# A transformer block with sliding-window attention: key-major scores, column-tiled PV, DMA layout changes and a list scheduler

## Chip, cores, metric

One core of a Trainium2 chip. The metric is the device time of one execution in microseconds, median of several runs.

## The reference

2048 tokens of 640 channels, all bf16; 32 heads of 20 channels; each query sees itself and the 255 keys before it; a gated MLP of width 1536. Shift, scale and gate vectors come from a vector `c` through `w_mod`.

```python
mod = (_silu(c) @ w_mod).reshape(c.shape[0], 6, 1, -1)      # sa, ca, ga, sb, cb, gb
h = _layernorm(x) * (1 + ca) + sa
q, k, v = h @ wqkv                                          # per head: 2048 x 20
scores = q @ k.T * 20 ** -0.5                               # masked to 0 <= i - j < 256
x = x + ga * ((softmax(scores) @ v) @ wo)
h = _layernorm(x) * (1 + cb) + sb
x = x + gb * ((_sigmoid(h @ w_gate) * (h @ w_up)) @ w_down)
```

## The kernel before

Tokens stand in 16 blocks of 128. A small planner (`Sched`) records each operation in program order on its engine, derives the semaphore waits, and emits five instruction streams; the order within an engine is the order of the Python code.

`ln1_stats` and `ln1_trans` normalise four blocks on VectorE (`xh`, L464), transpose them by TensorE matmuls with an identity into `ps_M`, and scale and shift them on the way out (`hT`, L492). `proj_tasks` computes Q and K transposed, with each head padded from 20 to 32 rows (`wq_pad`, `wk_pad`), so that head 4g + j of group g lies on partitions 32j to 32j + 19 (L590 evicts), and V with tokens on partitions, 22 columns a head, one of them ones (`vaug`, L605).

`attn_block(i)` handles one query block. For each four heads twelve score matmuls (three key blocks by four heads, L299) put keys on partitions: the stationary operand is a K block, 20 rows of one row group, the moving operand the 128 queries. ScalarE exponentiates two heads at a time (L730), GpSimd masks the far key block (L734), VectorE the diagonal one (L738). PV is query-major: the exponentiated block, 128 x 128, is stationary, V's 21 columns move, and three matmuls a head accumulate in `ps_O`. At the end of a block VectorE divides by the sums (L757, L758), TensorE transposes the result (L766), ScalarE evicts it (`oT`, L769), two groups of five matmuls apply `wo`, and VectorE adds the residual (L778).

The MLP of a chunk of four blocks (two for the last two chunks) starts after its attention: gate and up in 24 groups of five matmuls (L633 evicts gate by tanh, L640 multiplies), then down in two groups of twelve matmuls a block, a residual addition (L656) and the store (L660).

Attention and the rest are interleaved by hand: after each pair of heads `run_fill` takes one task from `fillq` (a projection group, a transpose, an MLP group) if it is due (`not_before` counts pairs). Nothing is left to take when `fillq` is empty or its tasks aren't due. All of `ps_M`'s users share two banks; the scores have four banks, PV two. Helper lines are L298 and L299 for all matmuls. All 31 DMAs are issued by SyncE: 15 loads at the start and one store a block.

Of the kernel before, what the change touches and what calls it, by code (L numbers as in the profile page):

```python
# [12 lines left out]

class Res:
    __slots__ = ("name", "w", "r", "psum")

    def __init__(self, name, psum=False):
        self.name = name  # L20
        self.w = None
        self.r = []
        self.psum = psum


class Op:
    __slots__ = ("fn", "waits", "skey", "inc", "tag")

    def __init__(self, fn, waits, skey, inc, tag=""):
        self.fn = fn  # L30
        self.waits = waits
        self.skey = skey
        self.inc = inc
        self.tag = tag


class Sched:
    ENG = ("pe", "act", "dve", "pool", "sp")
    ENGATTR = {"pe": "tensor", "act": "scalar", "dve": "vector", "pool": "gpsimd", "sp": "sync"}
    NDMA = 8  # L40

    def __init__(self, nc):
        self.nc = nc
        self.ops = {e: [] for e in self.ENG}
        self.cnt = {e: 0 for e in self.ENG}
        for k in range(self.NDMA):
            self.cnt[f"d{k}"] = 0
        self.cnt["out"] = 0
        self.dma_last = {f"d{k}": None for k in range(self.NDMA)}
        self.dma_rr = 0  # L50
        self.waited = {e: {} for e in self.ENG}
        self.tag = ""

    def add(self, eng, fn, reads=(), writes=(), signal=True, skey=None, inc=1, extra=()):
        key = skey or eng
        deps = {}

        def dep(ev, res=None):
            if ev is None:
                return  # L60
            k, v = ev
            if res is not None and res.psum and k == key:
                return
            if deps.get(k, 0) < v:
                deps[k] = v

        for r in reads:
            if r.w is None:
                raise RuntimeError(f"resource {r.name} read before any write (program order violation)")
            dep(r.w, r)  # L70
        for w in writes:
            dep(w.w, w)
            for ev in w.r:
                dep(ev, w)
        for ev in extra:
            dep(ev)
        waits = []
        wd = self.waited[eng]
        for k, v in deps.items():
            if k == key and v > self.cnt[k]:  # L80
                raise RuntimeError(f"engine {eng} depends on its own unsignaled op ({k},{v})")
            if wd.get(k, 0) < v:
                waits.append((k, v))
                wd[k] = v
        if signal:
            self.cnt[key] += inc
            ev = (key, self.cnt[key])
            op = Op(fn, waits, key, inc, self.tag)
        else:
            ev = (key, self.cnt[key] + inc)  # L90
            op = Op(fn, waits, None, 0, self.tag)
        self.ops[eng].append(op)
        for r in reads:
            r.r.append(ev)
        for w in writes:
            w.w = ev
            w.r = []
        return ev

    def dma(self, fn, reads=(), writes=()):  # L100
        k = f"d{self.dma_rr}"
        self.dma_rr = (self.dma_rr + 1) % self.NDMA
        prev = self.dma_last[k]
        ev = self.add("sp", fn, reads=reads, writes=writes, signal=True, skey=k, inc=16,
                      extra=([prev] if prev is not None else ()))
        self.dma_last[k] = ev
        return ev
# [38 lines left out]
D = 640  # L146
H = 32
# [734 lines left out]
```

## Time and profile before

| | |
|---|---|
| time, median of three runs | 559.47 us (559.28 to 560.45) |
| span of the profiled execution | 557.5 us |
| busy: PE, ACT, DVE, POOL | 423.9, 281.2, 262.8, 133.2 us |
| mean granted TensorE clock | 0.881 of 2.4 GHz |

The span runs from the first to the last instruction of one profiled execution; the time of a run takes in what lies around it. PE is TensorE's matmuls, PEld its weight loads (they overlap matmuls), DVE is VectorE, ACT ScalarE, POOL GpSimd, SP SyncE. The end of a matmul is modelled, so start to start tells more than a duration. A share is an average over stages with different limits.

### The profile page before, as it was taken

The page shows a single profiled execution, that of the slowest core. Times are in us where ns is not written, and L with a number is a line of the kernel's source. Part 1 is how long each engine was busy: PE and PEld are TensorE (multiplying, and loading weights), DVE is VectorE, ACT ScalarE, POOL GpSimd, SP SyncE. Part 2 cuts the span into 40 slices and gives each one's busy share as a digit, 9 for nine tenths or more (in the row PEclk, how much of TensorE's full clock was granted, in tenths as well). Part 3 has the DMA queues.
Part 4 walks back from the last instruction along what each step waited for, and adds up shares of the span by engine and source line. Part 5 has one row for each costly group of instructions (what it writes and reads, how often), then busy time and mean ns, then how long its engine had stood idle before and what let it go on. Part 6 is the DMA issues. An engine that isn't in the chain of part 4 may idle for free.

```text
span 557.5 us, 11493 instructions
## 1 busy us (share of the span) xinstructions
PE 423.9 (76%) x4784; PEld 254.3 (46%) x4828; DVE 262.8 (47%) x701; ACT 281.2 (50%) x441; POOL 133.2 (24%) x249
## 2 busy tenths in 40 slices
PE   0686789846597798985567889898557887984997
PEld 0333355424354454653344445655334445662665
DVE  5685432274473443435674444322844465445232
ACT  5112567755486666537355657267645564470120
POOL 4004800232222222314122313032323222230000
PEclk9987999975599999997558999999756999997899
DMA  8994000000000000010000000000000000100000
GB/s 288 358 393 162 1 2 1 1 1 2 2 1 1 1 1 2 14 36 1 1 1 1 2 1 1 25 25 2 2 1 1 1 2 2 36 13 1 1 25 25
DMA packets 12580, 20.07 MB, mean 36 GB/s; under 512 B 1136, under 2 KB 9968, under 8 KB 12528
## 3 DMA queue, kind: packets, MB, share of 16 engines
q1 hardware_dynamic: 12528, 19.34, 9.8%
q8 instruction: 38, 0.62, 0.4%
q14 instruction: 14, 0.11, 0.1%
HBM read 16.71 MB, written 2.62 MB: 35 GB/s over the span
## 4 chain that ended last, share of the span: by engine, by line
PE 59%; DVE 17%; ACT 13%; issue 7%; DMA 2%; POOL 1%; SPq 0%; ACTq 0%; POOLq 0%; DVEq 0%
PE ps_M L298 50%; ACT arena L730 8%; PE ps_S L299 6%; DVE stats L432 4%; PE ps_O L298 3%; DVE arena L738 2%; DMA arena<-in_w_mod_dram 2%; ACT oT L769 2%; DVE hT L492 2%; ACT arena L590 1%; DVE xh L464 1%; DVE arena L640 1%; PE ps_M L766 1%; DVE mvb L434 1%; POOL arena L734 1%
## 5 line engine op out<-in xcount | busy, mean ns | idle before, releaser
L730 ACT ACTIVATE arena<-ps_S 128x768 bf16<-128x768 f32 (+2 forms) x256 | 189.8, 768 | 100.9 <-PE ps_S L299 99.6
L734 POOL TENSOR_SCALAR_AFFINE_SELECT arena<-arena 128x256 bf16<-128x256 bf16 x224 | 109.7, 490 | 320.7 <-ACT arena L730 320.7
L738 DVE TENSOR_TENSOR arena<-arena,masku 128x256 bf16<-128x256 bf16 x256 | 81.5, 318 | 169.3 <-ACT arena L730 168.9
L298 PEld LDWEIGHTS ps_O<-vaug,arena 128*128 128x128 bf16 x1440 | 68.1, 100 | 56.2 <-DVE arena L738 15.6
L298 PE MATMUL ps_O<-vaug,arena 128*128 128x21 bf16 x1440 | 74.7, 176 | 18.6 <-DVE arena L738 13.4
L299 PE MATMUL ps_S<-arena 20*128 20x128 bf16 x1440 | 47.8, 239 | 36.9 <-ACT arena L730 30.6
L298 PE MATMUL ps_M<-h2T,wu_sb 128*128 128x512 bf16 (+1 forms) x294 | 64.0, 350 | 2.4 <-issue 0.8
L633 ACT ACTIVATE sig<-ps_M 128x512 f32<-128x512 f32 (+1 forms) x60 | 30.7, 512 | 69.7 <-PE ps_M L298 65.1
L298 PE MATMUL ps_M<-h2T,wg_sb 128*128 128x512 bf16 (+1 forms) x287 | 61.9, 347 | 4.8 <-DVE h2T L492 2.9
L590 ACT ACTIVATE arena<-ps_M 128x512 bf16<-128x512 f32 x64 | 38.2, 597 | 44.6 <-PE ps_M L298 43.8
L298 PE MATMUL ps_M<-wd_sb,arena 128*128 128x320 bf16 x384 | 55.6, 299 | 2.7 <-DVE arena L640 2.4
L299 PEld LDWEIGHTS ps_S<-arena 20*128 20x128 bf16 x1440 | 23.4, 99 | 54.6 <-ACT arena L730 38.3
L640 DVE SCALAR_TENSOR_TENSOR arena<-sig,ps_M 128x512 bf16<-128x512 f32 (+1 forms) x60 | 34.6, 577 | 20.0 <-PE ps_M L298 19.9
L298 PE MATMUL ps_M<-hT,wq_pad 128*128 128x512 bf16 x143 | 39.6, 407 | 5.6 <-DVE arena L738 1.7
L298 PEld LDWEIGHTS ps_M<-wd_sb,arena 128*128 128x128 bf16 x384 | 35.9, 98 | 17.6 <-DVE arena L640 3.2
L298 PE MATMUL ps_M<-hT,wk_pad 128*128 128x512 bf16 x152 | 40.8, 400 | 2.1 <-issue 0.8
L298 PE MATMUL ps_M<-wo_sb,oT 128*128 128x320 bf16 x160 | 29.8, 343 | 13.4 <-ACT oT L769 13.4
L298 PEld LDWEIGHTS ps_M<-h2T,wu_sb 128*128 128x128 bf16 x300 | 26.2, 101 | 23.3 <-DVE arena L640 5.0
L298 PEld LDWEIGHTS ps_M<-h2T,wg_sb 128*128 128x128 bf16 x300 | 26.8, 101 | 21.5 <-DVE h2T L492 2.1
L778 DVE TENSOR_TENSOR x_sb<-ps_M,x_sb 128x320 bf16<-128x320 f32 x32 | 15.7, 491 | 43.8 <-PE ps_M L298 43.8
L298 PE MATMUL ps_M<-ident,xh 128*128 128x128 bf16 x160 | 21.4, 267 | 19.4 <-DVE xh L464 5.3
L432 DVE BATCH_NORM_STATS2 stats<-x_sb 128x6 f32<-128x320 bf16 x64 | 31.0, 485 | 2.7 <-DMA x_sb<-in_A_x_dram 1.6
(56 smaller groups left out, 303.5 us busy)
## 6 DMA issues: line engine op xcount, KB each, us to landing
x_sb<-in_A_x_dram SPq DMA_DIRECT2D x4, 640.0 KB, 11.4
out_dram<-x_sb SPq DMA_DIRECT2D x16, 160.0 KB, 1.8
arena<-in_w_mod_dram SPq DMA_DIRECT2D x1, 2400.0 KB, 9.4
wg_sb<-in_B_w_gate_dram SPq DMA_DIRECT2D x1, 1920.0 KB, 16.7
wu_sb<-in_B_w_up_dram SPq DMA_DIRECT2D x1, 1920.0 KB, 18.0
wd_sb<-in_B_w_down_dram SPq DMA_DIRECT2D x1, 1920.0 KB, 21.1
arena<-in_A_wqkv_dram SPq DMA_DIRECT2D x2, 800.0 KB, 7.4
arena<-in_w_mod_dram SPq DMA_DIRECT2D x1, 1600.0 KB, 11.8
```

What stands on the lines that cost most here:

```text
L298: return lambda e: e.matmul(out_ap, l, r, start=start, stop=stop)
L299: return lambda e: e.matmul(out_ap, l, r, start=start, stop=stop, tile_position=tp)
L432: A("dve", lambda e, j=j: e.bn_stats(st[:, bi, j, :], src[:, j * 320:(j + 1) * 320]), reads=[R_x[b]], writes=[Rst_l[bi]])
L492: A("dve", (lambda e: e.tensor_scalar(dst_fn(dt), ps_M[:, m, 0:nblk * 128], sc1[:, sc_col0 + dt:sc_col0 + dt + 1], modcol[:, sh_col0 + dt: ...
L590: A("act", lambda e: e.activation(dstT[qs][:, g, :], ps_M[:, m, :], ACT.Copy), reads=[R_M[m]], writes=[Rdst[qs][g]])
L633: A("act", lambda e: e.activation(sig[ss][:, 0:ntok], ps_M[:, 0, 0:ntok], ACT.Tanh, scale=0.5), reads=[R_M[0]], writes=[R_sig[ss]])
L640: A("dve", lambda e: e.scalar_tensor_tensor(out=hhT[:, ft, 0:ntok], in0=sig[ss][:, 0:ntok], scalar=1.0, in1=ps_M[:, 1, 0:ntok], op0=ALU.ad ...
L730: A("act", lambda e, ss=ss, es=es, c0=c0: e.activation(E[es][:, :, c0:384], ps_S[:, 2 * ss:2 * ss + 2, c0:384], ACT.Exp, scale=SM_SCALE), ...
L734: A("pool", lambda e, es=es: e.affine_select(E[es][:, :, 0:128], E[es][:, :, 0:128], pattern=[[0, 2], [-1, 128]], compare_op=ALU.is_ge, fi ...
L738: A("dve", lambda e, es=es: e.tensor_tensor(E[es][:, :, 256:384], E[es][:, :, 256:384], masku[:].unsqueeze(1).to_broadcast([128, 2, 128]), ...
L769: A("act", lambda e: e.activation(oT[os_][:], Mb[:, 0:NDT * 128].rearrange("p (t q) -> p t q", t=NDT), ACT.Copy), reads=[R_M[0]], writes=[ ...
L778: A("dve", lambda e, m=m, n0=n0, n1=n1: e.tensor_tensor(x_sb[:, i, n0:n1], ps_M[:, m, 0:n1 - n0], x_sb[:, i, n0:n1], op=ALU.add), reads=[R ...
```

## The change

The kernel is written anew; the arithmetic is that of the reference as before.

- Order: each operation is given a duration, a priority and its reads and writes. `schedule` places operations one at a time on five engines at the earliest start by these durations, and among those that can start within 0.04 us takes the one of lowest priority number; the order so found is fixed in the instruction streams. Evictions may go to ScalarE or VectorE, whichever the list has free. Buffers are pools of slots given out in that order.
- Q and K are projected without padding (five row tiles of 128), evicted to a staging tile, written to a DRAM scratch and read back by four DMAs per half so that head j of a group lies on partitions from 32j.
- Attention runs over chunks of 2, 2, 4, 4, 2, 2 query blocks. For four heads and a set of key blocks, each score matmul has one key block stationary, as before, and all query blocks of the chunk that see it moving (128 to 384 columns); sets hold up to 512 columns a head. Two heads make one batch into one PSUM pair of banks, and one exp of up to 1024 elements a row follows. GpSimd applies both masks, four heads at a time.
- PV: V's 32 columns of a head are stationary in column tile j, the exponentiated keys move, and the output is O transposed, four heads on partitions 32j, with the sums in row 32j + 20. The output of 1024 columns is evicted as f32; the sums go to DRAM and back as 128 x 32, are inverted, go to DRAM and back as a broadcast, VectorE multiplies, and four DMAs write O without padding to DRAM, from which one DMA reads `oT` for the output projection.
- Layer norm: 1/sqrt by GpSimd's power; the transposes of all but the first four blocks by DMA (`dma_start_transpose`), scale and shift then in place on VectorE. `x` is loaded twice, once for each residual use.
- Modulation columns come from matmuls with one moving column each, gates from a broadcast silu. Eighteen matmuls of 512 columns on constant data stand at the start of TensorE's stream.
- MLP as before, by chunks of the new sizes; `ps_M` has three banks, the scores four, PV one.

New lines of the diff, cut to what the steps below speak of (the matmul, exp, mask and PV code replaces `attn_block`; `Sched`, `run_fill` and the padded weights go):

```diff
+                eps = 0.04
+                pick = min((x for x in lst if x[0] <= tmin + eps), key=lambda x: (x[1].prio, x[1].seq))
+                ent = (pick[0], e, pick[1])
+                if best is None or ent[0] < best[0]:
+                    best = ent
...
+CHUNKS = [2, 2, 4, 4, 2, 2]
...
+    p_E = sbpool("E", 4, [128, 4, 512])
...
+    p_S = Pool("S", [nc.alloc_psum_tensor(f"S{i}", [128, 2, 512], F32) for i in range(2)])
+    p_O = Pool("O", [nc.alloc_psum_tensor("O0", [128, 512], F32)])
+    p_M = Pool("M", [nc.alloc_psum_tensor(f"M{i}", [128, 512], F32) for i in range(3)])
...
+    def warm(e, g):
+        ins = None
+        for k in range(2):
+            ins = e.matmul(p_S.aps[0][:, 0, :], p_V.aps[0][:, 0:128], p_V.aps[0][:, 0:512], start=True, stop=True)
+        return ins
+    wprev = []
+    for i in range(9):
+        o = A("pe", warm, 0.85, prio=90, extra=p_V.init[0] + wprev, tag="warm", writes=[R("w")])
+        wprev = [o]
+    p_S.init[0].extend(wprev)
...
+    def transp(dst, src, bi, prio):
+        def fn(e, g):
+            return e.dma_start_transpose(dst.ap[:, :, bi * 128:(bi + 1) * 128], src.ap[:])
+        A("sp", fn, 1.2, reads=[src.r()], writes=[dst.r(("t", bi))], prio=prio, nbytes=163840 * 2, tag="transp")
...
+                evac(lambda s=s: s.ap[:], lambda ps=ps: ps.ap[:], 512, [ps.r()], [s.r()], 6, "evqk")
+                dma(lambda mt=mt, d=dt_: d[mt * 128:(mt + 1) * 128, :], lambda s=s: s.ap[:], 131072, reads=[s.r()],
+                    writes=[Rd[mt]], prio=2, tag="qkw")
...
+                for j in range(4):
+                    dma(lambda j=j, t=t: t.ap[32 * j:32 * j + DH, :, :],
+                        lambda j=j, hh=hh, d=dt_: d.rearrange("(g r) c -> r g c", r=4 * DH)[
+                            j * DH:(j + 1) * DH, 4 * hh:4 * hh + 4, :], 81920,
+                        reads=[Rd[m] for m in range(lo, hi + 1)], writes=[t.r(j)], prio=2, k=10, tag="qkr")
...
+    def pieces_of(i0, QB):
+        ps = []
+        for kb in range(max(0, i0 - 2), i0 + QB):
+            q0, q1 = max(kb, i0), min(kb + 2, i0 + QB - 1)
+            ps.append((kb, q0, q1 - q0 + 1))
+        ps.sort(key=lambda x: (-x[2], x[0]))
+        sets = []
+        for p in ps:
+            for s in sets:
+                if sum(y[2] for y in s) + p[2] <= 4:
+                    s.append(p)
                     break
...
+            else:
+                sets.append([p])
+        return sets
...
+            for si, st in enumerate(sets):
+                E = Tile(p_E, f"E{a}_{g}_{si}")
+                ncol = 128 * sum(p[2] for p in st)
+                for pr in range(2):
+                    Sp = Tile(p_S, f"S{a}_{g}_{si}_{pr}")
+
+                    def sc(e, eng, st=st, pr=pr, Sp=Sp, hh=hh, gl=gl, qt=qt):
+                        off = 0
+                        ins = None
+                        for (kb, q0, n) in st:
+                            kt = KT[(kb // 4, hh)]
+                            for jj in range(2):
+                                j = 2 * pr + jj
+                                ins = mm(e, Sp.ap[:, jj, off:off + n * 128],
+                                         kt.ap[32 * j:32 * j + DH, gl, (kb % 4) * 128:(kb % 4) * 128 + 128],
+                                         qt.ap[32 * j:32 * j + DH, gl, (q0 % 4) * 128:(q0 % 4 + n) * 128],
+                                         True, True, tp=(32 * j, 0))
+                            off += n * 128
+                        return ins
...
+                    A("act", lambda e, eng, E=E, Sp=Sp, pr=pr, ncol=ncol: e.activation(
+                        E.ap[:, 2 * pr:2 * pr + 2, 0:ncol], Sp.ap[:, :, 0:ncol], ACT.Exp, scale=SM_SCALE),
+                      c_act(2 * ncol), reads=[Sp.r()], writes=[E.r(pr)], prio=5, tag=f"exp{a}")
...
+                for which, o_ in [(0, x) for x in dg] + [(1, x) for x in fr]:
+                    def mk(e, eng, E=E, o_=o_, which=which):
+                        ap = E.ap[:, :, o_:o_ + 128]
+                        if which == 0:
+                            return e.affine_select(ap, ap, pattern=[[0, 4], [1, 128]], compare_op=ALU.is_ge, fill=0.0,
+                                                   base=0, channel_multiplier=-1)
+                        return e.affine_select(ap, ap, pattern=[[0, 4], [-1, 128]], compare_op=ALU.is_ge, fill=0.0,
+                                               base=-1, channel_multiplier=1)
+                    A("pool", mk, c_pool(512), reads=[E.r(0), E.r(1)], writes=[E.r((0, o_))], prio=5,
+                      tag=f"mask{a}")
...
+                def pv(e, eng, st=st, E=E, O=O, g=g, gcol=gcol, first=tuple(first)):
+                    off = 0
+                    ins = None
+                    fs = list(first)
+                    for (kb, q0, n) in st:
+                        for j in range(4):
+                            h = 4 * g + j
+                            oc = gcol + (q0 - i0) * 128
+                            ins = mm(e, O.ap[32 * j:32 * j + 32, oc:oc + n * 128], V[kb].ap[:, h * VW:h * VW + 32],
+                                     E.ap[:, j, off:off + n * 128], fs[j], True, tp=(0, 32 * j))
+                            fs[j] = False
+                        off += n * 128
+                    return ins
...
+        oT = Tile(p_oT, f"oT{a}")
+        dma(lambda: oT.ap[:, :, 0:W], lambda: doc.rearrange("(t p) c -> p t c", p=128), D * W * 2, reads=R_doc,
+            writes=[oT.r()], prio=2, tag="oT")
...
+        dma(lambda: dd[:], lambda: Oev.ap[DH:128:32, :, :].rearrange("p a b -> p (a b)"), 16384,
+            reads=[Oev.r(0), Oev.r(1)], writes=[R_dd], prio=1, k=4, tag="n_den")
+        Dn, Dr, Rb, On = Tile(p_Dn, "Dn"), Tile(p_Dr, "Dr"), Tile(p_R, "R"), Tile(p_On, "On")
+        dma(lambda: Dn.ap[:], lambda: dd.rearrange("j (q c) -> (j q) c", c=32), 16384, reads=[R_dd], writes=[Dn.r()],
+            prio=1, tag="n_denr")
+        A("dve", lambda e, g: e.reciprocal(Dr.ap[:], Dn.ap[:]), 0.45, reads=[Dn.r()], writes=[Dr.r()], prio=3,
+          tag="recip")
+        dma(lambda: dr.rearrange("j (q c) -> (j q) c", c=32), lambda: Dr.ap[:], 16384, reads=[Dr.r()], writes=[R_dr],
+            prio=1, tag="n_rw")
+        for j in range(4):
+            dma(lambda j=j: Rb.ap[32 * j:32 * j + DH, :], lambda j=j: dr[j:j + 1, :].to_broadcast([DH, 1024]), 81920,
+                reads=[R_dr], writes=[Rb.r(j)], prio=1, k=10, tag="n_rb")
+        A("dve", lambda e, g: e.tensor_tensor(On.ap[:], Oev.ap[:].rearrange("p a b -> p (a b)"), Rb.ap[:], op=ALU.mult),
+          c_dve(1024), reads=[Oev.r(0), Oev.r(1)] + [Rb.r(j) for j in range(4)], writes=[On.r()], prio=9, tag="onorm")
+        out_r = []
+        for j in range(4):
+            Rj = R(f"doc{nm}_{j}")
+            dma(lambda j=j: doc.rearrange("(g r) c -> r g c", r=4 * DH)[j * DH:(j + 1) * DH, g0:g0 + G, :],
+                lambda j=j: On.ap[32 * j:32 * j + DH, :].rearrange("p (g c) -> p g c", g=G), 40960, reads=[On.r()],
+                writes=[Rj], prio=1, k=10, tag="n_ow")
+            out_r.append(Rj)
+        return out_r
```

## Rows read from the trace of the kernel before

**Rows 1.** the page, busy us of each engine, and the granted clock in 40 slices.

```profile
PE 423.9 (76%) x4784; PEld 254.3 (46%) x4828; DVE 262.8 (47%) x701; ACT 281.2 (50%) x441; POOL 133.2 (24%) x249
...
PEclk9987999975599999997558999999756999997899
```

**Rows 2.** the page, the chain that ended last, shares by engine.

```profile
PE 59%; DVE 17%; ACT 13%; issue 7%; DMA 2%; POOL 1%; SPq 0%; ACTq 0%; POOLq 0%; DVEq 0%
```

**Rows 3.** busy time by stretch: us, PE (x), PEld, DVE, ACT, POOL, PEclk, DMA, GB/s.

```profile
120.00:160.00 40.00, 23.93 (x330) 14.66 (x327) 21.25 (x60) 19.45 (x28) 10.88 (x22) 0.55 0.00 1
160.00:200.00 40.00, 32.39 (x422) 18.99 (x416) 18.36 (x54) 28.35 (x44) 11.80 (x24) 1.00 0.01 2
200.00:250.00 50.00, 45.66 (x506) 27.44 (x510) 21.00 (x50) 24.88 (x37) 12.19 (x24) 1.00 0.04 15
250.00:300.00 50.00, 30.24 (x442) 19.02 (x441) 30.81 (x95) 26.64 (x38) 13.24 (x29) 0.62 0.00 1
330.00:370.00 40.00, 36.51 (x409) 22.40 (x412) 16.41 (x39) 19.05 (x29) 9.29 (x20) 1.00 0.05 18
370.00:430.00 60.00, 42.61 (x572) 25.57 (x575) 26.57 (x77) 37.37 (x56) 18.19 (x37) 0.74 0.01 1
```

**Rows 4.** who waited for whom: us in total, times, longest us.

```profile
ACT arena L730 <- PE ps_S L299: 99.6, 85, 12.5
```

**Rows 5.** timeline of PE, 251 to 254 us: start, us, engine, line, operation.

```profile
251.00 1.25 PE L298 MATMUL ps_M<-hT,wq_pad 128*128 128x512 bf16 x5
252.09 0.30 PE L298 MATMUL ps_O<-vaug,arena 128*128 128x21 bf16 x6
252.24 1.24 PE L298 MATMUL ps_M<-hT,wk_pad 128*128 128x512 bf16 x5
...
253.64 0.35 PE L299 MATMUL ps_S<-arena 20*128 20x128 bf16 x12
253.92 0.85 PE L298 MATMUL ps_M<-wv_sb,hT 128*128 128x320 bf16 x5
```

**Rows 6.** timeline of PE, 532 to 534 us, gate and up of two blocks.

```profile
532.38 0.72 PE L298 MATMUL ps_M<-h2T,wu_sb 128*128 128x256 bf16 x5
...
533.68 0.72 PE L298 MATMUL ps_M<-h2T,wu_sb 128*128 128x256 bf16 x5
```

**Rows 7.** timeline, 553 to 555 us, what follows each down group on DVE.

```profile
553.14 0.49 DVE L656 TENSOR_TENSOR x_sb<-ps_M,x_sb 128x320 bf16<-128x320 f32 x1 [1.14 <-PE ps_M L298]
554.77 0.49 DVE L656 TENSOR_TENSOR x_sb<-ps_M,x_sb 128x320 bf16<-128x320 f32 x1 [1.14 <-PE ps_M L298]
```

**Rows 8.** groups of ACT by form: line, shapes, count, busy us, mean ns, idle before.

```profile
L730 ACT ACTIVATE arena<-ps_S 128x768 bf16<-128x768 f32 x224 | 174.2, 808 | 84.0 <-PE ps_S L299 82.8
...
L633 ACT ACTIVATE sig<-ps_M 128x512 f32<-128x512 f32 x36 | 21.5, 597 | 27.8 <-PE ps_M L298 25.7 <-DVE arena L640 1.8 <-DVE arena L738 0.4
...
L730 ACT ACTIVATE arena<-ps_S 128x512 bf16<-128x512 f32 x16 | 9.5, 593 | 2.1 <-PE ps_S L299 1.9
L633 ACT ACTIVATE sig<-ps_M 128x256 f32<-128x256 f32 x24 | 9.2, 383 | 41.8 <-PE ps_M L298 39.4 <-DVE arena L640 2.2
```

**Rows 9.** groups of POOL by form, the two sizes of affine select.

```profile
L734 POOL TENSOR_SCALAR_AFFINE_SELECT arena<-arena 128x256 bf16<-128x256 bf16 x224 | 109.7, 490 | 320.7 <-ACT arena L730 320.7
...
L355 POOL TENSOR_SCALAR_AFFINE_SELECT masku<-arena 128x128 bf16<-128x128 bf16 x1 | 0.3, 292 | 0.1
```

**Rows 10.** the page, DMA issues: KB each, median us from issue to landing.

```profile
out_dram<-x_sb SPq DMA_DIRECT2D x16, 160.0 KB, 1.8
...
c_col<-in_c_dram SPq DMA_DIRECT2D x1, 1.2 KB, 2.8
```

**Rows 11.** timeline of SP's queue, first and last of the 15 loads.

```profile
0.80 0.44 SPq L311 DMA_DIRECT2D c_col<-in_c_dram  x1
...
28.66 3.48 SPq L348 DMA_DIRECT2D wd_sb<-in_B_w_down_dram  x1
```

**Rows 12.** timeline of PE, its first matmuls.

```profile
14.90 6.38 PE L298 MATMUL ps_M<-arena,siluc 128*1 128x320 bf16 x30 [14.90 <-DMA arena<-in_w_mod_dram]
```

More of the change, by code (lines that the diff above doesn't have):

```diff
@@ new lines, in build, with load_wm @@
+    x0 = {}
+    for b in range(4):
+        x0[b] = load_x(p_x0, b, 0.1 + 0.01 * b)
+    wm_src = w_mod.rearrange("(t p) f -> p t f", p=128)
+    def load_wm(i, prio, tmin=0.0):
+        t = Tile(p_big, f"wm{i}")
+        for kt in range(NDT):
+            dma(lambda kt=kt: t.ap[:].rearrange("p (t f) -> p t f", t=NDT)[:, kt, :],
+                lambda kt=kt: wm_src[:, kt, i * 1280:(i + 1) * 1280], 327680, writes=[t.r(kt)],
+                prio=prio + 0.01 * kt, tmin=tmin, tag=f"wm{i}")
+        return t
@@ new lines, in build @@
+    for q in range(4):
+        dma(lambda q=q: wd[:, 3 * q:3 * q + 3, :],
+            lambda q=q: B_w_down.rearrange("(t p) f -> p t f", p=128)[:, 3 * q:3 * q + 3, :], 491520,
+            writes=[R_wd[q]], prio=30, tmin=43 + 2.0 * q, tag="wd")
+    dma(lambda: wo[:], lambda: A_wo.rearrange("(t p) f -> p t f", p=128), 819200, writes=[R_wo], prio=29, tmin=22.0,
+        tag="wo")
+    A("act", lambda e, g: e.activation(cth[:], c_col[:], ACT.Tanh, scale=0.5), 0.2, reads=[R_ccol], writes=[R_cth],
+      prio=0)
@@ new lines, in build, with mm, pe_chain, fn @@
+    wprev = []
[3 more added lines that the diff above has]
+    p_S.init[0].extend(wprev)
+    def mm(e, o, l, r, st, sp, tp=None):
+        if tp is None:
+            return e.matmul(o, l, r, start=st, stop=sp, skip_group_check=True)
+        return e.matmul(o, l, r, start=st, stop=sp, tile_position=tp, skip_group_check=True)
+    def pe_chain(tile, n, pairs, reads, prio, tag, step=3, hold=(), gate=None, after=()):
+        i = 0
+        while i < len(pairs):
+            j = min(i + step, len(pairs))
+            if len(pairs) - j == 1:
+                j = len(pairs)
+            def fn(e, g, i=i, j=j):
+                ins = None
+                for k in range(i, j):
+                    o, l, r = pairs[k]()
+                    ins = mm(e, o, l, r, k == 0, k == len(pairs) - 1)
+                return ins
+            rd = {}
+            for k in range(i, j):
+                rd.update(dict.fromkeys(reads[k]))
+            if i == 0 and gate is not None:
+                rd.update(dict.fromkeys(reads[gate]))
+            o = A("pe", fn, sum(c_pe(n) for _ in range(i, j)), reads=list(rd), writes=[tile.r()], prio=prio, lat=0.25,
+              tag=tag, hold=hold if i == 0 else (), extra=after if i == 0 else ())
+            i = j
+        return o
```

1386 lines of the change are left out of this document (653 added, 733 removed).

## The prediction

> **What bounds the kernel now.** I read the page's shares first. PE is busy 423.9 us of 557.5, ACT 281.2, DVE 262.8, POOL 133.2 [rows 1]: no engine is full, and PE is nearest. The chain that ended last gives PE 59% [rows 2]. PE's granted clock in 40 slices [rows 1] falls to 5 or 6 tenths three times, so I read the stages next [rows 3]. From 160 to 250 and from 330 to 370 us the clock is 1.00 and PE is busy 32.39 + 45.66 + 36.51 of 130 us, 88.1%. From 120 to 160, 250 to 300 and 370 to 430 us it is idle 16.1 + 19.8 + 17.4 = 53.3 us, and at clocks of 0.55, 0.62 and 0.74 (between the levels 1.2 and 2.4 GHz) the busy time itself is stretched: a mean of 0.55 is 90% of the time at the lower level, which doubles work, so 0.9 x 23.93 / 2 = 10.8 us are lost, in the same way 11.5 and 11.1, together 33 us. There ACT waits for scores (99.6 us in all) [rows 4]: attention runs with no projection or MLP piece to fill PE. The kernel is bound by PE where it has fill, by attention's own ring (scores, exp, masks, PV) where it has none.
>
> **PE's work, piece by piece.** In one stretch at full clock [rows 5] I take start to next start, not the modelled end: five 512-column matmuls 251.00 to 252.09, so 0.217 us each; six PV matmuls 252.09 to 252.24, 0.15 us (their weights were loaded under the matmuls ahead); twelve scores 253.64 to 253.92, 0.28 us. Ten 256-column matmuls take 1.30 us [rows 6]; a down group of twelve 320-column ones 1.63, so 0.136 each [rows 7].
> - Q and K: the change drops the padding of 20 to 32 rows per head: 200 matmuls instead of 320, 43.4 us instead of 69.4.
> - V and the output projection: 320 of 320 columns on either side, 43.5 us.
> - Gate and up: chunks of 2, 2, 4, 4, 2, 2 blocks instead of 4, 4, 4, 2, 2: 240 x 0.217 + 480 x 0.130 = 114.5 us instead of 109.3.
> - Down: 384 x 0.136 = 52.2 us, unchanged.
> - Transposes: 240 of 128 columns (0.054 us each by the 512 row) become 20: 1.1 us instead of 13. The other 28 block transposes go to DMA.
> - Modulation: 20 x 0.136 plus 100 one-column matmuls that no row shows; between nothing and 0.13 each, I take half: 9 us.
> - Scores: 832 wide matmuls instead of 1440, but the same 184,320 columns, two row groups per batch: 38.4 us at 2.4 GHz. The old batch of twelve needs 3 x 0.053 = 0.16 us with four row groups at once and takes 0.28, so 0.12 us go to changing over or to issue. If each of 208 batches pays that, 63; if batches pair up, 38, and with four row groups at once 19. I take 51, against 33.6 now.
> - PV: now 240 x 0.15 = 36 us. After, 184,320 columns in 32-column tiles, which no row shows. Four at a time, as the row tiles of [rows 5] run: 19, with 0.12 for each of 104 batches 32. One at a time 77 + 12 = 89. I take 32, since the row tiles are the nearest thing, and keep 19 and 89.
>
> The Trainium skill ("TensorEngine Tiling (Array Packing)", Key Properties) says that changing the tiling mode drains TensorE. That speaks against a change which mixes row tiles, column tiles and whole-array fill: by it all 312 tiled batches pay the 0.12, 95 us for scores and PV instead of 83, and the time below grows by 14. The 0.12 agrees in kind, but the trace can't tell a drain from issue.
>
> Sum after: 43.4 + 43.5 + 114.5 + 52.2 + 1.1 + 9 + 51 + 32 = 347 us, against 366 counted the same way for before. So PE gets only some 20 us less work; the gain must come from the 133.6 us in which PE is idle and the 33 at low clock.
>
> **The other engines.** Exp has the same elements: 16 of 768 a row at 0.808, 144 of 1024 (0.215 per 256 more, so 1.02), 48 of 512 at 0.593 = 188 us [rows 8], as before. Tanh 24 x 0.597 + 48 x 0.383 = 33. The Q/K, V and O evictions (104, at most 0.6, 58 us) go to ACT or DVE, whichever the list has free. ACT carries 221 to 279 us. DVE loses its 256 diagonal masks. POOL takes both masks: 240 of 512 elements; 256 take 0.490 and 128 take 0.292 [rows 9], extrapolated 0.89, or 0.65 if POOL's fixed part is as large as its rough spans allow: 156 to 213 us, plus 17 weight scalings of 1.4. All stay under PE's 347, so ACT and POOL have slack where fill is spread evenly. That is what list order and smaller chunks can do: no separate "attention alone" stage is left, since PE order mixes 268 us of fill into 221 us of ACT work, and a late MLP covers the next attention.
>
> **What is added: DMA.** I count 396 issues on SP instead of 31: 16 normalisations of 11 (denominators out, in; reciprocals out; four broadcasts in; four writes out), 40 + 64 for Q and K, 28 transposes, 66 loads, 6 O reads, 16 outputs. An output of 160 KB lands in 1.8 us, a load of 1.2 KB in 2.8 [rows 10]; an issue takes 0.44 us with an empty queue [rows 11]. From the last PV of a chunk to its output projection six transfers follow each other: 6 x 2.25 + 2 x 3 x 0.45 more issues = 16 us, plus eviction, reciprocal and product, about 19. SP waits in order: behind a wait for a landed denominator stand loads, Q/K reads and transposes of later chunks. In the middle of the kernel PE has other work over those 19 us; after the last chunk it has not: 19 + projection 3 + norm 5 + transposes 4 + MLP 23 + store 2 = 56 us, of which MLP of the chunk ahead (22), its own projection and MLP fill all but some 15. The price if the cover is gone everywhere is rival C.
> No row shows a DMA transpose. From below, a plain 160 KB transfer: 0.45 + 1.8 us. From above, the scattered c load (640 two-byte pieces, 1.0 us more than the large output): 1.6 ns an element, 131 us a block. I take 4 us, next to the row of equal bytes; far beyond it, rival D is the case.
> The Trainium skill ("VectorE: DVE Perf Modes", The three transpose paths) states 1309 ns for 128 x 128 by the DMA crossbar: five of them 6.5 us a block, and with it the tail grows by some 5 us. No run here shows it so far.
>
> **The sum.** 347 / 0.881 (PE's share in the three stages that have fill at full clock) = 394. In front, PE's first real work: before it starts at 14.9 us [rows 12], after 1600 KB of Q and K weights that the change puts behind the modulation weights; I take 13. Tail idle 15. Together 422 of span; the median 559.47 lies 2.0 above the span 557.5, so **424 us**. Of the 135 gained, PE work is 20, low clock 33, idle 82.
> Own range: scores 38 and PV 19 give 322 / 0.913 (the best stage) + 13 + 9 + 2 = 377; PE 359 (scores 63) at the share of 160 to 200 us, 0.81, gives 443 + 30 = 473.
>
> **The rivals.**
> - B, column tiles don't overlap: PV 89 instead of 32, 57 / 0.881 = 65 more: 489. For: no column tile is in the trace. Against: row tiles overlap in it. 0.13.
> - C, PE stands at each chunk's first output projection until the DMA chain is through: PE is in order, so a chain later than the list assumed stops MLP and scores too. Six chunks x 19, half covered: 57 more, 481. For: one queue, fixed order. Against: 1.8 us landing is short. 0.12.
> - D, slower: SP becomes the bound. The 15 loads at the start hold SP 22.8 us in sum, first and last in [rows 11], 1.5 us each, since an issue is long when transfers stand in front or need many pieces. 396 x 1.5 = 594, + 15 to start and the rest of the tail: 620. It decides from a mean of about 1.0 us a transfer (396 us) and loses against before from 1.36. Slow transposes would come in here. Against: most are 16 to 80 KB on an empty queue. 0.14.
> - E, order and clock don't change: the list's order stalls as much as the old one does: 559 - 20 = 540. 0.03.
>
> **How the numbers follow.** Forecast 0.58, B 0.13, C 0.12, D 0.14, E 0.03. The range takes in the forecast's lower bound and B with some width: 380 to 500; outside are D, E and the forecast's ends. About 0.2% (1 us) is what a measurement tells from no change: faster 0.85, same 0.01, slower 0.14.
>
> **What will show it.** PE busy near 370 with a clock over 0.95; no stage with PE under 75% between 30 us and the last 40; exp about 1.02 us; masks 0.65 to 0.89. A PV batch of 512 columns that holds PE for 0.3 us means four at a time, 0.85 means B. PE waiting for the O transfer tens of us in sum means C; SP busy most of the span means D. I am wrong in kind if PE's clock stays low because attention still runs alone, or if ACT is full while PE waits.

## The result, and the profile after

| | before | after |
|---|---|---|
| device time, median (all runs), us | 559.96 (559.28 to 561.74, 4 runs) | 405.79 (402.35 to 412.31, 4 runs) |
| ratio after / before | | 0.7187, 95% interval 0.7167 to 0.7207 |
| the profiled execution: time; span, us | 559.47; 557.5 | 402.93; 401.2 |
| TensorE busy; idle in the span, us | 423.9; 133.6 | 378.9; 22.3 |

The kernel became 154 us faster by the medians: 405.79 us lies 18 us below the 424 us forecast, and inside its range. The ratio, and the differences between kernels below, go by a kernel's executions within 1.5% of its fastest; for the changed kernel these are 402.35 and 402.93 us (mean 402.6, granted clock 0.957), not 408.65 and 412.31 us (0.941 and 0.929).

The page of the changed kernel, busy us of each engine, granted clock in 40 slices, chain that ended last:

```profile
PE 378.9 (94%) x3419; PEld 190.0 (47%) x3446; DVE 205.9 (51%) x425; ACT 232.3 (58%) x317; POOL 200.4 (50%) x295
...
PEclk9898999656999999999899999999999999999999
...
PE 79%; DMA 6%; ACT 3%; SPq 3%; issue 3%; DVE 3%; POOL 2%; DVEq 0%; ACTq 0%; POOLq 0%
```

Against [rows 1, 2] PE's busy time fell by 45 us only, its idle time by 111; the chain is 79% PE where it was 59%. By stretch (columns as in [rows 3]):

```profile
40.00:80.00 40.00, 36.99 (x387) 13.57 (x389) 21.92 (x42) 31.17 (x43) 23.98 (x38) 0.91 0.65 181
80.00:120.00 40.00, 37.56 (x361) 13.83 (x361) 25.63 (x54) 33.10 (x38) 30.87 (x47) 0.79 0.97 256
120.00:160.00 40.00, 38.54 (x369) 17.61 (x373) 26.17 (x46) 30.03 (x36) 35.39 (x46) 1.00 0.43 119
...
200.00:240.00 40.00, 40.00 (x447) 20.41 (x445) 20.17 (x43) 32.83 (x47) 26.44 (x40) 1.00 0.23 64
...
360.00:400.00 40.00, 38.39 (x328) 31.72 (x325) 15.23 (x37) 8.87 (x24) 0.00 (x0) 1.00 0.10 27
```

No stage is left like the three of [rows 3] in which PE stood idle 29 to 40% of the time: from 40 us to the end it is busy 92 to 100% of every 40 us, the tail among them. One new thing shows: the clock is down from 72.8 to 96.7 us, though PE is busy 89% of 75 to 95 us.

How the pieces run, a stretch of PE's timeline at full clock (start, modelled duration, operation), then two weight loads of it:

```profile
204.90 0.39 PE L509 MATMUL S<-QT,KT 20*128 20x384 bf16 x4
205.22 0.40 PE L509 MATMUL O<-E,V 128*32 128x256 bf16 x8
205.56 0.72 PE L508 MATMUL M<-wd,big 128*128 128x320 bf16 x4
206.21 0.39 PE L509 MATMUL S<-QT,KT 20*128 20x384 bf16 x4
...
209.78 1.26 PE L508 MATMUL M<-wd,big 128*128 128x320 bf16 x8
210.98 0.39 PE L509 MATMUL S<-QT,KT 20*128 20x384 bf16 x4
```

```profile
205.22 0.12 PEld L509 LDWEIGHTS O<-E,V 128*32 128x32 bf16 x8 [0.21 <-issue]
205.55 0.39 PEld L508 LDWEIGHTS M<-wd,big 128*128 128x128 bf16 x4 [0.21 <-issue]
```

Starts are what to read. A score batch (512 columns, two heads at once: 0.213 us of streaming) holds PE 0.32 us. A PV batch of the same columns, its four column tiles at once, holds it 0.34; one at a time would be 0.85. Four down matmuls of 320 columns take 0.65 between tiled batches, eight take 1.20, where [rows 7] give 0.136 each, 0.54 and 1.09. So every change of tiling costs 0.107 to 0.127 us in these rows, on the way into tiles and on the way out (0.107 is taken below). In the last two rows no weight load runs for 0.21 us ahead of the change, so the first one after it is not hidden under the matmuls before it. Counted along the timeline there are 472 changes, 188 into score batches, 100 into PV batches and 184 back to the full array: some 50 us.

### The profile page after: what moved, and what is told of

It is laid out like the page before. It is cut to its first block, busy times and chain, and to the rows that moved or that the text cites. A ratio compares the mean times of both kernels' runs of the same rounds, so it can differ in the third digit from the quotient of the medians.

```text
span 401.2 us, 9280 instructions
## 1 busy us (share of the span) xinstructions
PE 378.9 (94%) x3419; PEld 190.0 (47%) x3446; DVE 205.9 (51%) x425; ACT 232.3 (58%) x317; POOL 200.4 (50%) x295
## 4 chain that ended last, share of the span: by engine, by line
PE 79%; DMA 6%; ACT 3%; SPq 3%; issue 3%; DVE 3%; POOL 2%; DVEq 0%; ACTq 0%; POOLq 0%
PE M L508 61%; PE S L509 12%; PE O L509 6%; ACT E L750 3%; SPq L431 2%; DMA oT<-doc 2%; DMA big<-in_w_mod_dram 1%; DMA KT<-dk 1%; POOL E L766 1%; DMA R<-dr 1%; DVE hT L598 1%; DMA hT<-x 1%; POOL E L768 1%; SPq L593 1%; DVE Oev L642 1%
## 5 line engine op out<-in xcount | busy, mean ns | idle before, releaser
L750 ACT ACTIVATE E<-S 128x1024 bf16<-128x1024 f32 (+1 forms) x208 | 182.9, 909 | 35.8 <-PE S L509 31.4
L766 POOL TENSOR_SCALAR_AFFINE_SELECT E<-E 128x512 bf16<-128x512 bf16 x128 | 84.2, 667 | 67.9 <-ACT E L750 52.2
L871 ACT ACTIVATE sig<-M 128x256 f32<-128x256 f32 (+1 forms) x72 | 32.8, 455 | 89.2 <-PE M L508 89.1
L509 PE MATMUL S<-QT,KT 20*128 20x256 bf16 (+2 forms) x832 | 76.7, 272 | 3.0 <-ACT E L750 1.9
L768 POOL TENSOR_SCALAR_AFFINE_SELECT E<-E 128x512 bf16<-128x512 bf16 x112 | 75.1, 677 | 0.0
L873 DVE SCALAR_TENSOR_TENSOR big<-sig,M 128x256 bf16<-128x256 f32 (+1 forms) x72 | 36.7, 510 | 74.8 <-PE M L508 62.4
L508 PE MATMUL M<-h2T,wu 128*128 128x256 bf16 (+1 forms) x356 | 67.9, 308 | 1.2 <-ACT sig L871 0.7
L508 PE MATMUL M<-h2T,wg 128*128 128x256 bf16 (+1 forms) x354 | 66.5, 308 | 1.5 <-issue 1.4
L508 PE MATMUL M<-wd,big 128*128 128x320 bf16 x384 | 56.6, 300 | 0.0
L508 PEld LDWEIGHTS M<-wd,big 128*128 128x128 bf16 x384 | 36.0, 98 | 16.9 <-issue 2.5
L509 PE MATMUL O<-E,V 128*32 128x256 bf16 (+2 forms) x832 | 40.1, 275 | 2.6 <-POOL E L768 2.1
```

The lines of the kernel that those rows point to most:

```text
L508: return e.matmul(o, l, r, start=st, stop=sp, skip_group_check=True)
L509: return e.matmul(o, l, r, start=st, stop=sp, tile_position=tp, skip_group_check=True)
L750: A("act", lambda e, eng, E=E, Sp=Sp, pr=pr, ncol=ncol: e.activation(E.ap[:, 2 * pr:2 * pr + 2, 0:ncol], Sp.ap[:, :, 0:ncol], ACT.Exp, sca ...
L766: return e.affine_select(ap, ap, pattern=[[0, 4], [1, 128]], compare_op=ALU.is_ge, fill=0.0, base=0, channel_multiplier=-1)
L768: return e.affine_select(ap, ap, pattern=[[0, 4], [-1, 128]], compare_op=ALU.is_ge, fill=0.0, base=-1, channel_multiplier=1)
L871: A("act", lambda e, g, pg=pg, sg=sg: e.activation(sg.ap[:, 0:W], pg.ap[:, 0:W], ACT.Tanh, scale=0.5), c_act(W), reads=[pg.r()], writes=[s ...
```

## The experiments

**What a change of tiling costs by itself.** Nine sequences of matmuls on constant data, which wait for nothing, stand in place of the eighteen warm-up matmuls:

```diff
-    def warm(e, g): ...            # 2 matmuls, nine times
+    SEG = [(40, [F2]), (20, [S2]), (20, [S4]), (20, [P4]), (12, [F2, F2, S2]), (12, [F2, F2, S4]),
+           (12, [F2, F2, P4]), (12, [S2, P4]), (12, [F2, F2, S2, P4])]
```

> The changed kernel with its eighteen warm-up matmuls replaced by nine runs of matmuls on constant data, and the first gate group of a chunk put behind the last down group of the chunk before; the extra matmuls feed nothing. F is a full-array matmul of 512 columns, S a score batch (two heads in two row tiles, 512 columns), S4 the same with four heads in four row tiles, P a PV batch of four column tiles, 512 columns. Theory (a change of tiling costs about 0.107 us in either direction, because the first weight load after it starts only when the matmuls before it are through): at full clock a run of F alone, S alone, S4 alone or P alone costs 0.213 each, F F S costs 0.64 + 0.21 = 0.85, F F S4 and F F P the same, S P 0.64, F F S P 1.17. Rival 1 (only the way into tiles costs): F F S 0.75, S P 0.64 or 0.53. Rival 2 (the bubble seen in the changed kernel is a wait on semaphores and not a change of tiling): no sequence here waits for anything, so F F S 0.64 and S P 0.43.

PE's timeline, in three of the nine (this kernel took 485.32 us, executed once):

```profile
36.37 0.60 PE L498 MATMUL M<-V 128*128 128x512 bf16 x2
36.91 0.39 PE L505 MATMUL S<-V 20*128 20x512 bf16 x2
37.23 0.61 PE L498 MATMUL M<-V 128*128 128x512 bf16 x2
...
58.34 0.60 PE L498 MATMUL M<-V 128*128 128x512 bf16 x2
58.88 0.40 PE L511 MATMUL O<-V 128*32 128x512 bf16 x4
59.21 0.60 PE L498 MATMUL M<-V 128*128 128x512 bf16 x2
...
67.79 0.39 PE L505 MATMUL S<-V 20*128 20x512 bf16 x2
68.11 0.40 PE L511 MATMUL O<-V 128*32 128x512 bf16 x4
68.44 0.39 PE L505 MATMUL S<-V 20*128 20x512 bf16 x2
```

F F S takes 36.37 to 37.23, 0.86 us; F F P 0.87; S P 0.65; F F S P, further on, 1.19; the theory said 0.85, 0.85, 0.64, 1.17. Both rivals are out: the price is there without any wait, and in both directions. F F S4, with four row tiles, takes 0.865 on the mean of twelve: twice the scores in the same time. The Trainium skill ("TensorEngine Tiling (Array Packing)", Key Properties) says that changing the tiling mode drains the engine; the run agrees, and sets the price at 0.11 us.

The same run shows the clock. From 13.08 to 26.91 us PE ran score batches and nothing else (120 matmuls, no idle), then PV batches (PE busy, PEclk, DMA):

```profile
12.00:16.00 4.00, 4.00 (x34) 1.00 1.06 377
16.00:20.00 4.00, 4.00 (x42) 0.57 0.37 126
24.00:28.00 4.00, 4.00 (x34) 0.50 0.00 0
28.00:32.00 4.00, 4.00 (x60) 0.73 0.01 4
32.00:36.00 4.00, 4.00 (x34) 1.00 0.00 0
```

A fully busy engine fell to 1.2 GHz while it ran only batches of 20 rows, and came back to 2.4 GHz while it ran PV batches of 128 rows (from 26.91 us). The Trainium skill ("TensorE: Matmul & The Clock Gate", HAM oscillation — how this bites in real kernels) puts such a fall down to gaps in which the engine waits; this one came without a gap.

**Without the filling.** The first score batch of a chunk waits for the MLP of the chunk before:

```diff
+        if a:
+            last["s"] = last["s"] + [last["res2"]]
         oT = attention(a, i0, QB)
```

> The changed kernel, with one wait more: the first score batch of a chunk waits for the last residual of the MLP of the chunk before, so that no MLP or out projection runs beside attention; only Q, K and V projections still do. Same instructions otherwise. Theory (the gain is the filling of TensorE during attention, not less work): the MLP and the out projection, some 165 us of streaming, go behind the attention chunks instead of into them, and each of six chunks adds its normalization chain and its ACT-bound attention without cover: 560 to 660 us, no better than the kernel before. Rival (the gain is cheaper instructions): at most 440 us.

664.62 us (661.04 to 668.2), slower than before by 19% (17.9 to 19.5%). Page and PE's waits (us in total, times, longest):

```profile
PE 448.0 (68%) x3446; PEld 215.5 (33%) x3446; DVE 187.4 (28%) x395; ACT 245.8 (37%) x347; POOL 191.3 (29%) x295
```

```profile
PE M L508 <- DMA oT<-doc: 89.2, 6, 19.7
PE M L508 <- DVE h2T L598: 50.8, 5, 13.0
```

The same instructions without overlap lose more than the whole gain. Against the changed kernel's profile PE is idle 189 us longer and busy 69 us longer, at a granted clock of 0.723: the filling is worth idle time and clock. The chain of transfers after a chunk, which I had put at 19 us, is here in the open: 89.2 us in six waits, 14.9 on the mean, the longest 19.7.

**More work for PE.** Three matmuls more in each Q/K group, same order:

```diff
+                for k in range(pad if i == 0 else 0):
+                    o, l, r = pairs[k]()
+                    mm(e, o, l, r, True, True)
```

> The changed kernel in the same order of instructions, with three matmuls of 512 columns more at the head of each of the forty groups of the Q and K projections; their result is overwritten. 120 matmuls of 0.213 us are 25.6 us more on TensorE. Theory (TensorE's stream is the bound from the first scores to the end): 20 to 27 us longer, the ten groups of the first chunk partly lost in waits for weights. Rival (ACT, GpSimd or a chain of DMAs sets the end and TensorE has slack): under 8 us.

423.05 us (422.71 to 424.28), 20 more than the changed kernel's 402.6; the profiled span is 20.0 longer (421.2), PE's busy time 25.4:

```profile
PE 404.3 (96%) x3566; PEld 201.3 (48%) x3566; DVE 205.5 (49%) x425; ACT 231.9 (55%) x317; POOL 201.5 (48%) x295
```

PE is the bound: 20 of 25.4 us come out in the total. The rest went into idle time, 16.9 us instead of 22.3.

**A longer chain of DMAs.**

```diff
+        dma(lambda: doc2[:], lambda: doc[:], D * W * 2, reads=R_doc, writes=[R_doc2], prio=2, tag="hop")
```

> The changed kernel with one more copy from DRAM to DRAM of the normalized O of each of the six chunks before it is read back transposed, some 4 to 6 us each on the chain that leads from attention to the out projection; the order is planned again with it. Theory (the chain is covered by MLP work of the chunk before): 0 to 5 us longer in all, most of it at the last chunk. Rival C of the prediction (TensorE stands at each chain): six times 4 to 6 us, 25 to 35 us longer.

417.54 us (415.75 to 417.82): 15 more, between the two forecasts. The page shows where:

```profile
PE 391.9 (95%) x3446; PEld 192.2 (46%) x3446; DVE 207.7 (50%) x427; ACT 231.6 (56%) x315; POOL 198.6 (48%) x295
...
PEclk9798999555999599999999999779999999999999
```

PE's idle time is 414.0 - 391.9 = 22.1 us, as without the copy: the chain is covered, and C is out. What grew is busy time at a lower clock (mean 0.926 instead of 0.957, 13 us busy more for the same matmuls). So the order, which was planned again, counts through the clock, which neither theory had.

**Cheaper scores, fewer changes, and what the planner knows.** Three kernels whose planner counts 0.107 us for each change of tiling: the first is the control, the second makes one score batch of the two in a set (four row tiles) and gives scores and exps the priority number 1, where they had 10 and 5, the third also makes one PV batch for a head group.

```diff
+                dur += 0.107 if md(o) != pem[0] else 0.0       # all three
-                for pr in range(2):                            # second and third
-                    Sp = Tile(p_S, f"S{a}_{g}_{si}_{pr}")
+                Sp = Tile(p_S, f"S{a}_{g}_{si}")               # four banks, j in range(4)
+                if si < len(sets) - 1:                         # third
+                    continue
```

> The changed kernel with two edits to its planner and none to the work: a change of tiling on TensorE is counted with 0.107 us in the planned times, and the first gate group of a chunk is put behind the last down group of the chunk before. It has 456 changes of tiling in its order, where the changed kernel has 472. It is also the control for the two kernels planned in the same way beside it. Theory (TensorE's stream sets the time, and this order has nearly the same stream): within 5 us of the changed kernel. Rival (the order itself is worth much, since the planner worked with wrong durations): 8 us or more faster.

> The control, with the two score batches of a set (two heads each) made one: four heads in four row tiles onto the four score banks at once, 104 batches instead of 208, two exps on each as before. The score banks are now one buffer and no longer two, so the scores of a set wait for both exps of the set before. In the run with constant data four row tiles streamed in the time of two. Theory (TensorE's stream is the bound, and half of the score stream and some 90 changes of tiling are waste): half of some 39 us of pure score streaming and 89 times 0.107, 29 us in all, less what ACT loses by the single buffer: 12 to 30 us faster than the control. Rival (ACT, now without a second buffer, becomes the bound during attention): no faster, or slower by up to 104 times 0.5 us.

> The kernel with merged score batches, and besides the PV batches of all sets of a head group (one to three) made one, issued when the last set has its masks: 277 changes of tiling instead of 367, at the same streaming. Theory (each change costs 0.107): 90 times 0.107, 5 to 10 us faster than the merged kernel. Rival (TensorE waits for the masks of whole groups, and the four E buffers run out): no faster.

The control came out at 444.43 us (441.24 to 459.26; 442.49 by the rule above), 40 slower than the changed kernel: my expectation fell, and the rival's too. The merged scores gave 396.17 (393.92 to 398.82), the third kernel 392.93 (390.58 to 395.67), ratio to before 0.7015 (0.6971 to 0.7059): the fastest here. Against the control, of which its forecast speaks, the merged kernel is 46 us faster and not 12 to 30, because the control fell back; the third is 3 us faster than the second and not 5 to 10, in ranges that overlap. Pages of the first two, in this order, and waits of PE in the second, cut to those for masks and exps:

```profile
PE 419.4 (92%) x3420; PEld 197.5 (43%) x3446; DVE 212.8 (47%) x431; ACT 228.5 (50%) x311; POOL 199.0 (43%) x295
...
PEclk9799998757555599999855558999899999999999
```

```profile
PE 345.9 (88%) x3419; PEld 180.8 (46%) x3446; DVE 206.8 (53%) x421; ACT 228.2 (58%) x321; POOL 201.6 (51%) x295
...
PE O L516 <- POOL E L775: 14.2, 19, 2.2
PE S L516 <- ACT E L756: 6.1, 7, 1.3
```

Merging takes 33 us of busy time from PE against the changed kernel; 19.2 us of score streaming and 105 changes fewer, 11.2 us, make 30 of them. Yet it takes only 6 from the total: idle time doubles, from 22 to 46 us. PE's waits for masks are 14.2 us, where the changed kernel has 2.1, those for exps 6.1 instead of 1.9. That the single score buffer causes this is argued and not shown, since the priorities changed too. The control is the other lesson: in its profiled execution (459.26 us) span 457.5 and busy 419.4 leave 38 us idle, 16 more; the busy time is 40 us longer for nearly the same stream, at a clock of 0.851.

**Is it the clock?** One useless full-array matmul ahead of each score batch: of the second chunk of the changed kernel, and of the third and fourth chunk of the control (orders kept).

```diff
+                        for _ in range(1 if a == 1 else 0):      # control: if a in (2, 3)
+                            mm(e, Sp.ap[:, 0, :], ident[:], wq[:, 0, 0:512], True, True)
```

> The changed kernel in the same order, with one full-array matmul of 512 columns on resident data more at the head of each of the 32 score batches of the second chunk (its result is overwritten by the scores). That is the stretch from about 60 to 90 us, where the changed kernel had only score and PV batches on TensorE, and the granted clock was 0.5 from 75 to 95 us. It adds 6.8 us of streaming and up to 64 changes of tiling, 6.8 us. Theory (the clock falls where TensorE has only tiled batches, and ACT, 94% busy there, sets the pace of that stretch): the clock stays at or near 1 there, and the total stays within 6 us. Rival 1 (the low clock itself costs its full half of 22 us): 5 to 10 us faster. Rival 2 (the clock falls from something else, such as the idle gaps before it): still 0.5 there, and 10 to 20 us slower.

> The kernel with the price in its planner (the one that came out at 444 us), in the same order, with one full-array matmul of 512 columns on resident data more at the head of each of the 96 score batches of the third and fourth chunk; its result is overwritten by the scores. These are the stretches where that kernel had a granted clock of 0.5 (110 to 160 us and 230 to 270 us of its trace) with TensorE 97 to 100% busy. It adds 20 us of streaming and some changes of tiling. Theory (its 40 us over the changed kernel are the clock, which falls and stays low where full-array matmuls are too thin among the tiled batches, and not its order or its stream): the clock comes back to near 1 there, which gives back some 50 us, and the total falls to 410 to 430 us although there is more work. Rival 1 (the order costs it, by waits): 20 to 30 us slower, 465 or more. Rival 2 (full-array matmuls don't matter to the clock): still 0.5 there, 470 or more.

The changed kernel (first fence) has no full-array matmul from 71.3 to 90.2 us, and a clock of 0.50 in each 5 us from 75 to 95; with the added ones (second fence) it is 1.00 to 90 us (columns as in [rows 3]):

```profile
75.00:80.00 5.00, 4.74 (x52) 1.27 (x52) 1.57 (x3) 4.79 (x7) 4.35 (x8) 0.50 0.52 149
```

```profile
75.00:80.00 5.00, 4.35 (x53) 1.53 (x54) 2.47 (x5) 4.74 (x7) 3.54 (x6) 1.00 0.47 123
```

The profiled execution (404.26 us) has a span 1.3 us longer than the changed kernel's, and its clock did what the theory said. The other three took 412 to 417 us at mean clocks of 0.943 to 0.958, against 0.979, and have no trace: that the clock stays up there every time is not shown. The median of the four is 412.79 us; 404.26 against 402.6 is "within 6 us". Rival 1 is out: the second chunk's scores end 31.6 us after the first's, against 28.0 at low clock. ACT is busy 87 to 97% of 70 to 90 us either way, so a faster PE had little to win there.

Rival 2 is less clear than its forecast made it. In the changed kernel the clock fell at 72.8 us, right behind a wait for a mask:

```profile
72.40 0.40 PE L509 MATMUL O<-E,V 128*32 128x256 bf16 x8 [0.73 <-POOL E L768]
```

The added matmuls closed such gaps too: from 70 to 75 us PE is busy 4.72 us instead of 3.75. So this pair does not tell thin full-array work from a gap. The run with constant data does, for score batches alone: there was no gap in it.

The control, profiled at 459.26 us (first fence, clock 0.851), and the control with added matmuls, at 439.49 us (second, 0.942), by PE's busy time, PEclk and DMA:

```profile
110.00:130.00 20.00, 19.67 (x128) 0.51 0.72 194
```

```profile
110.00:130.00 20.00, 20.00 (x195) 1.00 0.93 283
...
210.00:230.00 20.00, 17.96 (x184) 0.58 0.19 52
```

The clock is 1.00 in every 20 us from 90 to 210, the stretch that has the added matmuls, and falls right behind it: the fourth chunk's scores end at 206 us, and it is low from 213.1 to 250.6. From the end of the second chunk's scores to that of the fourth's the control takes 98.3 to 219.4 us, this kernel 89.5 to 205.7: 4.9 us less, with 20 us of streaming more. In that stretch the control ran at half clock from 110.2 to 161.4 us, 51.2 us, half of which is 25.6. So in this execution the low clock made the control slow there. The two profiles are the longest of the control's times and the shortest of this kernel's, so 4.9 is no figure for their medians.

The median, 448.74 us (439.49 to 453.2), is not below the control's. Rival 1's 465 and rival 2's 470 and clock of 0.5 are out, and so are my 410 to 430: the added work and the low clock behind it took back what the clock gave. That all 40 us of the control are clock is not shown. An estimate from its own times: 441.24 us at a mean clock of 0.899 and 459.26 at 0.851 are 18 us for 0.048, so the 0.058 up to the changed kernel's 0.957 are worth some 22 of the 40.

**An even order.** Two score buffers, one PV batch for a head group, 0.09 us a change in the planner.

```diff
+                if si < len(sets) - 1:
+                    continue
+                dur += 0.09 if md(o) != pem[0] else 0.0
```

> The changed kernel with its two score buffers, its score batches of two heads and the PV batches of a head group made one (412 changes of tiling), planned with 0.09 us for each change, an order in which full-array matmuls are spread evenly over attention: in only 6 us of it do they fill less than four tenths of a stretch of 8 us, in the changed kernel in 32 us, in the one at 444 us in 118 us. Theory (TensorE's stream and its clock set the time, and an even spread keeps the clock): clock 0.97 or more, 60 changes of tiling fewer than the changed kernel, 385 to 400 us. Rival (the gaps of the PV batches that wait for whole groups eat it): 400 us or more.

397.19 us (393.94 to 405.36), 7 less than the changed kernel (395.86 against 402.6), where 60 changes fewer are worth 6.4. Time and, in three executions, clock (0.970 to 0.974) are as the theory forecast. The profiled one, 405.36 us, had 0.941: it was low from 56.6 to 73.6 and from 128.2 to 145.3 us, although full-array matmuls took about half of the time there. Each fall came behind a wait of PE for a transfer of K or Q:

```profile
55.25 0.34 PE L516 MATMUL S<-QT,KT 20*128 20x256 bf16 x4 [2.65 <-DMA KT<-dk]
...
126.64 0.81 PE L515 MATMUL M<-hT,wk 128*128 128x512 bf16 x3 [1.82 <-DMA dq<-stg]
```

So in the whole kernel thin full-array work and gaps come together, and which of them brings the clock down is not separated. Left open is also why the clock, once low, stays low at a mixture at which it elsewhere stays high.

## Why the prediction was right, and where its sizes were off

**The bound.** Right: most of the gain is idle time, 133.6 to 22.3 us, 111 where 82 were forecast. The clock gave some 26: over the whole span it costs the changed kernel 15.6 us (from windows of 20 and 40 us, worked as in the prediction), the old one some 42, since outside the prediction's three stages, with their 33, it was low too, as here in the old kernel:

```profile
480.00:520.00 40.00, 29.74 (x338) 21.13 (x336) 18.65 (x54) 14.07 (x24) 6.97 (x14) 0.84 0.04 14
```

PE's work at full clock fell from 382 to 363 us, by 19 where 20 were forecast. That this came out is partly luck: both of the prediction's sums, 366 and 347, are some 16 us too low. Without the filling the kernel takes 665 us. Which part of the change makes the filling possible (the list's order, the smaller chunks, the layout by DMA) no run separates.

**PE's stream, 347 us predicted.** At full clock, by the prices that the runs show, it is 363:

| piece | predicted | worked out | how |
|---|---|---|---|
| scores | 51 | 58.5 | 38.4 + 188 x 0.107; 20 batches follow one of their kind |
| PV | 32 | 29.9 | 19.2 + 100 x 0.107 |
| back to the full array | 0 | 19.7 | 184 x 0.107 |
| matmuls on constant data | 0 | 3.8 | 18 x 0.213, left out of the prediction's sum |
| gate and up | 114.5 | 104.6 | 256 columns: five in 0.55, not 0.65 |
| modulation | 9 | 6.7 | one column: 0.04 us each |
| Q, K, V, wo, down, transposes | 140.2 | 140.2 | unchanged, by [rows 5, 7] |

With 15.6 us of clock that is 379, against 378.9 busy; a change costs up to 0.127 us and not always 0.107, so agreement to a few us is all that this shows. The step that was mis-sized is the 0.12 us of [rows 5]: I charged it on the way into tiles, for half of the score batches and all PV batches, and nothing on the way back. Scores, PV and the way back are 108 us, where I had 83. The sum that I had weighed against it, 95 by the rule of the Trainium skill, was nearer, but it too was charged on tiled batches alone.

[Rows 6] gave 0.130 for a matmul of 256 columns. The ten there are two groups, and the second stood behind a pause: 532.38 to 532.93 and 532.93 to 533.68 us, 0.55 and 0.75. Five in a row take 0.55 in the changed kernel too:

```profile
379.15 0.71 PE L508 MATMUL M<-h2T,wu 128*128 128x256 bf16 x5
379.70 0.71 PE L508 MATMUL M<-h2T,wg 128*128 128x256 bf16 x5
380.24 0.71 PE L508 MATMUL M<-h2T,wu 128*128 128x256 bf16 x5
```

The eighteen matmuls on constant data stand in the first 37 us, between other work, and not all at the start of the stream (twelve run from 2.46 to 7.8 us).

**Idle time, 75 us predicted** (47 of 394 - 347, 13 in front, 15 in the tail): 22.3 idle + 15.6 clock = 38. This was the larger miss, 37 us the other way; with the stream 16 us too small the two in part cancel, and the span misses by 21 only: that much is luck. I took PE's share in the best stages of the old kernel, 0.881; the changed kernel keeps PE busy 92 to 100% of every 40 us, in the tail too (38.39 of the last 40 us), where I expected 15 us of standing.

**The other engines.** ACT's exp of 1024 takes 1.024 us (1.02 predicted), POOL's masks 0.667 and 0.677 (0.65 to 0.89):

```profile
L750 ACT ACTIVATE E<-S 128x1024 bf16<-128x1024 f32 x144 | 143.7, 1024 | 24.8 <-PE S L509 20.9 <-PE O L509 1.3 <-POOL E L766 0.3
...
L766 POOL TENSOR_SCALAR_AFFINE_SELECT E<-E 128x512 bf16<-128x512 bf16 x128 | 84.2, 667 | 67.9 <-ACT E L750 52.2 <-PE M L508 9.6 <-PE S L509 5.2
```

ACT carries 232 us, inside 221 to 279.

**DMA and the rivals.** Block transposes on SP (ns, min/median/max), two pieces of the chain (start, us), and PE's wait for the transposed O:

```profile
L593 SPq DMA_TRANSPOSE h2T<-x x16: 1205/1236/1491, 109.0 to 373.8; - x16
```

```profile
30.59 1.45 SPq L593
32.14 2.65 DMA hT<-x
```

```profile
PE M L508 <- DMA oT<-doc: 0.6, 1, 0.6
```

A block of 128 x 640 holds SP 1.24 us. In the chain the third of the first four takes 1.45 us of issue; the fourth, issued at 32.14 us, has landed at 34.79, 2.65 us with its own issue. I took 4 us. The 6.5 us worked out from the Trainium skill ("VectorE: DVE Perf Modes", The three transpose paths) are farther off. B is out (PV 0.34). C is out: PE waits for the transposed O once, 0.6 us, and the copy that made the chain longer added no idle time. D is out: the 396 issues hold SP 186 us in sum, 0.47 us each, where D needed about 1.0, and add 3% to the chain that ended last. E is out. The chain after a chunk was sized right for its longest case, 19.7 us where nothing covers it.

**What I had not foreseen** is the clock: I expected it above 0.95 because attention never runs alone. It is 0.957 in the profiled run, but falls where attention does run alone on PE, from 72.8 to 96.7 us, and in another order of the same work PE was busy 40 us longer at 0.851.

## What to carry to other kernels

When a change fills an engine's idle time, check the fill itself by taking it away, and size the filled engine by its stream plus the price of switching between kinds of work, both ways; here 472 changes at 0.107 us, some 50 us, cost more than streaming all scores, 38 us. Give row tiles all four row groups at once before counting on them, and look at the waits that the lost buffer may bring. Compare orders by the granted clock as well as by idle time: a list planned with the measured price of a change was 40 us slower.

## What the runs showed of the hardware

- A change between full-array, row-tiled and column-tiled matmuls costs about 0.11 us in either direction, with nothing to wait for (F F S 0.86 us where the streaming is 0.64, S P 0.65 where it is 0.43).
- Four row tiles of 20 rows stream in the time of two (F F S4 0.865, F F S 0.86 us).
- TensorE's clock fell from 2.4 to 1.2 GHz under score batches alone with the engine 100% busy, and came back under column-tiled batches of 128 rows. In the one traced execution each of two kernels it stayed at 1.00 (75 to 90 us; 90 to 210 us) when one full-array matmul of 512 columns was put ahead of each score batch.
- DMA transposes of 128 x 640 in two-byte elements held their queue 1.24 us in the median of the sixteen of the second layer norm; one at the start landed 2.65 us after its issue began.
